# Retention and SwiGLU on one core: where stores are issued, which engine scales and copies pairs 8 to 11, and how many sums stand ahead of the first product

## The chip, the cores and the metric

The kernel runs on one NeuronCore of a Trainium2 chip, as one launch. The metric is the device time of that launch in microseconds (us). The engines are TensorE (PE; its weight loads are listed as PEld), VectorE (DVE), ScalarE (ACT), GpSimd (POOL) and SyncE (SP). SP computes nothing here, it only issues transfers; ACT issues transfers as well, between its computations. Each engine works through its own instructions in order. An instruction waits for semaphores, and whatever stands behind it on its engine waits too.

## The reference

Two blocks follow each other, all in float32.

```
B, H, S, D = 8, 8, 576, 64
scores = (q @ k.T) / sqrt(D)
ret    = scores * gamma[h] ** (i - j)  where i >= j, else 0     # gamma[h] = 1 - 2 ** (-5 - h)
x      = (ret @ v), heads side by side                          # 4608 tokens x 512
g, val = x @ w_gate, x @ w_val                                  # 512 x 1536 each
out    = (g * sigmoid(g) * val) @ w_out                         # 1536 x 512
```

## The kernel before

**Retention.** The 8 batches times 4 pairs of heads are 32 pairs, pair i = 4b + p. A sequence is cut into nine chunks of 64; within a chunk the masked scores are used, and between chunks a 64x64 state per head is carried. `tick(t)` is one beat of a pipeline over the pairs. On PE it issues, in this order, `own_values(t-2)` (masked scores times v), `new_states(t-1)` (keys times v), `earlier_values(t-2)` (state times q) and `scores(t-1)`. The work of the other engines is put into the list `pieces` and taken from it one by one by `go_on`: `masked(t-1)` gives `copies` (one copy of half the new states out of PSUM, tile `even`), `own` (mask times scores, tile `ret`) and `states` (`ret_last`, then the running sum over the chunks, tile `state`); `transposes(t)` gives `keys` (keys times their decay) and two DVE transposes of q and k; `to_x(t-2)` gives `outputs`, which move the result out of PSUM into x. Three predicates choose engines. `whole(i)` chooses a layout. `vector(i)` puts the `keys` of pair i and the `copies` one pair earlier on DVE instead of ACT, and moves `keys` behind the transposes. `light(i)` lets ACT multiply q by its decay before the transpose (`scale_q`, line 480), so that `outputs` are plain copies on ACT; for other pairs the decay is multiplied in by DVE when x is written (lines 597 and 611). `needed(1)` is 14, `needed(2)` is 22 and `FIRST` is 12.

**The feed-forward part** works on tiles of tokens. Tile 0 has 512 tokens and plain matmuls: `up0(f)` for the 12 column blocks f of w_gate and w_val (line 695), then `down0(f)` (line 707), which adds into four PSUM banks A, B, C, E, and `out0`, which copies the banks out and stores the first 512 rows. Tiles 1 to 4 have 1024 tokens each. For them a block product of 32 smaller products is done with 26, at the price of sums before and after. The tables `UP` and `DOWN` hold one line per product: the bank, the operand slots, and the sums. There are three quarters qd of 26 steps for the up side (`up_step`, four matmuls a step, line 924) and 26 steps for the down side (`down_step`, line 963). In tile 1 the sums of the weights are made on the way: `first_sums` and `w_sums` (POOL, with sign changes on ACT, lines 892, 893 and 902) before a step, after which ACT stores the summed weight block to DRAM (line 927) for tiles 2 to 4. `x_sums` makes the sums of x (DVE in tile 1, line 731 through `add`). Fourteen of tile 1's 22 sums of x stand ahead of step 0 (`X_FIRST_OF_ALL`), and one more ahead of each step. `reads` takes the result out of the bank: an ACT copy (line 861) or a DVE sum with the bank (line 864). ACT's Silu (line 939) and a product by DVE (lines 942 and 945) or POOL follow. Steps 0 to 3 and 10 and 11 are read by ACT copies, steps 4 to 9 by DVE. A line marked "+" adds onto what its bank holds: step 7 adds onto step 4's bank, step 8 onto step 5's, step 9 onto step 6's, and so on, and may begin when that bank has been read.

**The sums of w_out** (`out_sums`, table `OUT_SUMS`) are 26 operands of 128x256 for each of three quarters. Each is summed if need be (24 sums a quarter) and stored to DRAM (line 782), and is read back from there by the down steps of all later tiles. Quarters 0 and 1 are POOL's, its sums go to `pool_places` and SP stores them. The third quarter is DVE's, its sums go to `vector_places`, and ACT stores them. The 22 vector places are eight in the old x (`x0_places`, used once), six in the raw weight buffer and eight in `part`. A place whose value is no longer needed goes to the end of the list (`release`, `free`), so the 23rd and 24th sums get places that an earlier sum has used, and wait until that sum has been stored.

**Order.** Instructions of every engine stand in the order in which the Python code runs (`manual_schedule`). The loop over `down_order` calls `down0`, then `go_on(6)`; at m = 1, 3, 6 and 8 ticks 10 to 13; at m = 8 the `first_sums` of quarter 0; from m = 9 the first `x_sums`; then a group of three stores with their sums from POOL's list and a group of three from DVE's. Then come `out0`, six more `x_sums` and the 26 steps of quarter 0, with `load(12)` issued in program order after step 6 and `load(13)` after step 14. `load(i)` fetches q, k and v of pair i, ten transfers on SP; for pair 11 they are ACT's. The tile framework gives each transfer one of eight semaphores, and a transfer waits until the one before it on its semaphore has landed, whichever engine issued it.

Of the kernel before, what the change touches and what calls it, by code (L numbers as in the profile page):

```python
# [154 lines left out]
def kernel(  # L155
# [291 lines left out]

    def light(i):

        return needed(1) - 2 <= i < needed(2) - 2  # L450

    def vector(i):

        return i == 0 or 10 <= i <= needed(1) - 2

    def transposes(i):
        p = i % HP
        qk, kn, vt = loaded.pop(i)
        qT = early[i] if i < HP else qp.tile([P, S], F32, tag="qT", name="qT")
        st[i] = dict(qT=qT, kn=kn, v=vt)  # L460
        pieces = []

        copy = nc.scalar.copy if i else nc.vector.tensor_copy
        if i < HP:

            for n, (t, src, bank) in enumerate(((kT, kn, bankB), (qT, qk, bankA)) if i else ((qT, qk, bankA), (kT, kn, bankB))):
                for c in range(NFULL):
                    nc.tensor.transpose(bank[:, ts(c, P)], src[:, ts(c, P)], ident)
                for hl in range(2):
                    nc.tensor.matmul(bankC[half[hl], ts(n, L)], src[half[hl], CW : CW + D], ident[half[hl], half[hl]],  # L470
                                     start=True, stop=True, skip_group_check=True)
                copy(t[:, 0:CW], bank)
                copy(t[:, CW:S], bankC[:, ts(n, L)])
        else:
            if light(i):
                def scale_q():

                    src = qk[:, 0].rearrange("p (j r) d -> p r j d", r=2)
                    for r in range(2):
                        nc.scalar.activation(out=src[:, r], in_=src[:, r], func=AF.Copy, scale=piece[:, 2 * p + r : 2 * p + r + 1])  # L480
                pieces.append(scale_q)
            for n, t in enumerate((qT, kT)):
                pieces.append(lambda n=n, t=t: nc.vector.transpose(out=t, in_=qk[:, n].rearrange("p j d -> p (j d)")))

        every = slice(0, P)

        def keys():
            blocks = kn.rearrange("p (g d) -> p g d", d=D)
            if i < HP:
                parts = [(0, every, blocks[:, 0 : NC - 1 : 2]), (1, every, blocks[:, 1:NC:2]), (1, half[1], blocks[half[1], NC - 1])]  # L490
            elif whole(i):
                parts = [(0, every, blocks[:, 0:NFULL]), (1, every, blocks[:, NFULL:NC])]
            else:
                parts = [(hl, every, blocks[:, hl : 2 * NFULL : 2]) for hl in range(2)]
            for hl, rows, at in parts:
                scale = key[rows, 2 * p + hl : 2 * p + hl + 1]
                if vector(i) or 1 < i < HP:
                    (nc.vector if vector(i) else nc.gpsimd).tensor_scalar(out=at, in0=at, scalar1=scale, scalar2=None, op0=ALU.mult)
                else:
                    nc.scalar.activation(out=at, in_=at, func=AF.Copy, scale=scale)  # L500

        if light(i):
            return [lambda: (keys(), pieces[0]())] + pieces[1:]
        if vector(i) and i:
            return [lambda: None] + pieces + [keys]
        return [keys] + pieces

    straight, exchanged = [(slice(0, P), slice(0, P))], [(half[0], half[1]), (half[1], half[0])]
# [129 lines left out]
    def tick(t, lo=HP, hi=NP, spread=False, then=None):  # L638
        go_on(len(pieces))
        if hi == HP:  # L640

            if lo <= t - 1 < hi:
                scores(t - 1, True)
                new_states(t - 1)
                for f in masked(t - 1):
                    f()
            if t + 1 == HP:
                split(0)
                rounding(0)
            if lo <= t - 2 < hi:  # L650
                own_values(t - 2)
            for f in transposes(t) if lo <= t < hi else ():
                f()
            if t + 1 == HP:
                rounding(1)
            if lo <= t - 2 < hi:
                earlier_values(t - 2)
                to_x(t - 2)[0]()
            return
        if lo <= t - 2 < hi:  # L660
            own_values(t - 2)
        if lo <= t - 1 < hi:
            new_states(t - 1)
        if lo <= t - 2 < hi:
            earlier_values(t - 2)
        if lo <= t - 1 < hi:
            scores(t - 1, t - 2 < lo)
        if lo <= t - 1 < hi and whole(t - 2) and not whole(t - 1):
            decay(slice(0, H), slice(0, H), half[1])
        copies, *masks = masked(t - 1) if lo <= t - 1 < hi else (lambda: None,)  # L670
        keys, *new = transposes(t) if lo <= t < hi else (lambda: None,)
        outputs = to_x(t - 2)[0] if lo <= t - 2 < hi else lambda: None
        if t - 2 >= 0 and light(t - 2):
            pieces.append(lambda: (copies(), keys(), outputs()))
        else:
            pieces.extend([lambda: (copies(), keys()), outputs])
        pieces.extend(masks)
        pieces.extend(new)
        if then:
            pieces.append(then)  # L680
        if not spread:
            go_on(len(pieces))
# [25 lines left out]
                             start=(f == down_order[0]), stop=(f == down_order[-1]))  # L708

    def out0():  # L710
        for i, bank in enumerate(banks):
            o = rest[:, part_at + 512 * i : part_at + 512 * (i + 1)]
            (nc.vector.tensor_copy if i > 1 else nc.scalar.copy)(out=o, in_=bank)
        for i in range(4):
            nc.scalar.dma_start(out=out[i * P : (i + 1) * P, :], in_=rest[:, part_at + 512 * i : part_at + 512 * (i + 1)])


    up, down = lines(UP), lines(DOWN)
# [25 lines left out]
    for line in OUT_SUMS:  # L744
        i, s = line.split("|")
        slot, ops = s.split(":")
        events += [(int(op[1]), op) for op in terms(ops)] + [(None, int(slot), int(i))]

    def out_sums(qd):


        place = {}

        def free(p):
            if not any(p is q for q in x0_places):
                sum_places.append(p)

        eng, queue, sum_places = ((nc.vector, nc.scalar, vector_places) if qd + 1 == NQ else (nc.gpsimd, nc.sync, pool_places))

        def view(s):  # L760
            return w_dn[:, qd, s // 2, s % 2] if s < 8 else place[s]

        def used(e):
            return [e[1]] if e[0] is None else [int(a) for a in e[1][2:]]

        def release(k):

            for s in list(place):
                for e in events[k + 1 :]:
                    if s in used(e):  # L770
                        break
                    if s == e[0]:
                        free(place.pop(s))
                        break
                else:
                    free(place.pop(s))

        def do(k):
            e = events[k]
            if e[0] is None:  # L780
                _, slot, i = e
                queue.dma_start(out=dn_ops[i][:, qd * TB : (qd + 1) * TB], in_=view(slot))
            else:
                new = sum_places.pop(0)
                add(eng, e[1], view, new)
                if e[0] in place:
                    free(place[e[0]])
                place[e[0]] = new
            release(k)

        r, ends = [], [k for k, e in enumerate(events) if e[0] is None]
        for g in range(0, N, 3):
            lo, hi = ends[g - 1] + 1 if g else 0, ends[min(g + 2, N - 1)] + 1

            def group(lo=lo, hi=hi):
                for k in range(lo, hi):
                    do(k)

            r.append(group)
        return r  # L800
# [43 lines left out]
        rested.append(b)  # L844
        return banks[b]

    silus = [0]

    products = []

# [24 lines left out]

    x_ops = [op for line in up for op in line[3]]
    X_FIRST = 8
    X_FIRST_OF_ALL = 14

    def x_sums(n, lo, hi, vector):  # L880
        for op in x_ops[lo:hi]:
# [26 lines left out]
    def up_step(n, qd, i):  # L908
        label, opens, xslot, _, wslot, _, ops = up[i]
        busy = n == 1  # L910
        if qd == 0:
            first = X_FIRST_OF_ALL if busy else X_FIRST
            x_sums(n, first + i, first + i + 1, busy)
        if busy:
            if i > 1:
                w_sums(qd, i)
# [4 lines left out]
        b = bank(label, i == 0)  # L921
        for gv in range(2):
            for c in range(2):
                nc.tensor.matmul(b[:, gv * TB : (gv + 1) * TB], w[:, gv, ts(c, P)], rhs[:, c, :],  # L924
                                 start=(opens and gv == 0 and c == 0), stop=(c == 1), skip_group_check=True)
        if busy:
            nc.scalar.dma_start(out=up_ops[qd][i].rearrange("p (g x) -> p g x", g=2), in_=w)
            if i in (22, 25) and qd + 1 < NQ:
# [112 lines left out]
    for m, f in enumerate(down_order):  # L1041
        down0(f)
        go_on(6)
        if m in tick_at:
            tick(tick_at[m], HP, FIRST, tick_at[m] + 1 < needed(1))
            go_on(1)
        if m == 8:
            first_sums(0, 0, 4)
        if m > 8:
            x_sums(1, 3 * (m - 9), min(3 * (m - 8), X_FIRST), True)  # L1050
        if groups:
            groups.pop(0)[1]()
        if last_groups:
            last_groups.pop(0)()
    out0()
    x_sums(1, X_FIRST, X_FIRST_OF_ALL, True)
    done = FIRST

    def spread_tick(t):
# [3 lines left out]
    for n in range(1, NTILE):  # L1063
# [3 lines left out]
        if n == 1:  # L1067

            for i in range(N):
                ups.pop(0)()  # L1070
                if i in (6, 14):
                    load(FIRST + i // 14)
        downs = [lambda i=i: down_step(n, i) for i in range(N)]
        merge((0.0, ticks(done, cut)), (0.5, ups))
# [38 lines left out]
```

## Time and profile before

| what | us |
|---|---|
| median of 11 runs (lowest to highest) | 1061.25 (1059.79 to 1063.21) |
| the profiled execution's own time | 1060.36 |
| its span in the trace | 1058.6 |
| busy in the span: PE, DVE, POOL, ACT | 1038.2, 656.8, 391.3, 273.1 |
| PE from 40 to 160 us | busy throughout |
| tile 0's `up0`, then `down0` | to 124.7, then 127.3 to 179.7 |
| tile 1's first step | 180.14 |

The granted TensorE clock is 1.0 throughout. The 1.76 us between span and own time lie outside the traced instructions, and the own time is 0.89 us under the median. Times are counted from the start of the span. A line of the timeline reads: start, duration, engine (with a q: the engine's issue of transfers), line of the code, operation, what it writes and reads, count, and in brackets the engine's idle time before it and what ended that. Busy time of PE is modelled from pipelined matmuls, so that only the bracketed gaps tell where PE stood still.

### The profile page before, as it was taken

The numbers are of one execution on the slowest core, as the hardware profiler recorded it, in microseconds if no ns is written. First come the engines' busy times: TensorE is split into PE (matmuls) and PEld (weight loads), VectorE is DVE, ScalarE is ACT, GpSimd is POOL, SyncE is SP. The second block draws the span as 40 slices with busy tenths as digits, with TensorE's granted clock in tenths as the row PEclk, the third lists the DMA queues.
The fourth block names the chain that finished last, engine by engine and source line by source line (L and its number), as shares of the span: only waits on it lengthen the run. The fifth ranks groups of instructions, "written<-read, shape, count | busy, mean of one in ns | idle before, by whom it ended". The sixth has DMA issues, their size and how long they took to land.

```text
span 1058.6 us, 21426 instructions
## 1 busy us (share of the span) xinstructions
PE 1038.2 (98%) x8448; PEld 850.4 (80%) x8448; DVE 656.8 (62%) x1094; ACT 273.1 (26%) x579; POOL 391.3 (37%) x338
## 2 busy tenths in 40 slices
PE   7999999999999999999999999999999999999998
PEld 6454555788788888888888888888888888888887
DVE  4568778686878667454467787426375654244644
ACT  4555400332533211231312112232220022232110
POOL 2002357665455107622224038412250383122505
PEclk9999999999999999999999999999999999999999
DMA  9998787747768869755766777544554454555543
GB/s 264 253 255 250 183 252 208 226 159 187 189 177 218 265 168 245 212 147 173 192 189 169 210 197 212 154 145 141 157 175 150 154 187 151 152 155 161 181 159 99
DMA packets 305082, 199.08 MB, mean 188 GB/s; under 512 B 219992, under 2 KB 248664, under 8 KB 304984
## 3 DMA queue, kind: packets, MB, share of 16 engines
q1 hardware_dynamic: 269528, 157.19, 54.2%
q10 hardware_dynamic: 35456, 40.54, 11.4%
q8 instruction: 67, 1.10, 0.4%
q14 instruction: 31, 0.25, 0.1%
HBM read 157.56 MB, written 40.11 MB: 187 GB/s over the span
## 4 chain that ended last, share of the span: by engine, by line
PE 84%; DVE 6%; DMA 3%; POOL 3%; issue 2%; ACT 1%; SPq 1%; ACTq 0%; DVEq 0%; POOLq 0%
PE bankC L924 11%; PE bankA L924 11%; PE bankB L924 11%; PE bankE L924 11%; PE bankA L963 6%; PE bankE L963 6%; PE bankB L963 6%; PE bankC L963 6%; DVE rest L864 3%; PE bankA L695 2%; PE bankC L695 2%; PE bankB L695 2%; PE bankE L695 2%; POOL rest L731 2%; PE outer L546 2%
## 5 line engine op out<-in xcount | busy, mean ns | idle before, releaser
L864 POOL TENSOR_TENSOR rest<-rest 128x512 f32<-128x512 f32 x56 | 79.1, 1419 | 297.3 <-DVE rest L864 276.3
L939 ACT ACTIVATE io<-rest 128x256 f32<-128x256 f32 x180 | 75.0, 417 | 338.8 <-DVE rest L864 288.1
L924 PE MATMUL bankA<-rest,arena 128*128 128x256 f32 x544 | 129.1, 380 | 2.2 <-ACT rest L861 1.4
L924 PE MATMUL bankC<-rest,arena 128*128 128x256 f32 x544 | 129.2, 380 | 1.2 <-POOL arena L893 0.7
L731 POOL TENSOR_TENSOR arena<-arena 128x512 f32<-128x512 f32 (+1 forms) x72 | 114.3, 1600 | 26.7 <-DMA up<-arena 17.9
L924 PE MATMUL bankE<-rest,arena 128*128 128x256 f32 x512 | 121.5, 380 | 0.5 <-DVE rest L864 0.5
L924 PE MATMUL bankB<-rest,arena 128*128 128x256 f32 x512 | 121.4, 380 | 0.4 <-DVE rest L864 0.4
L924 PEld LDWEIGHTS bankA<-rest,arena 128*128 128x128 f32 x544 | 102.8, 190 | 18.1 <-issue 2.1
L924 PEld LDWEIGHTS bankC<-rest,arena 128*128 128x128 f32 x544 | 102.8, 190 | 16.3 <-issue 1.2
L946 POOL TENSOR_TENSOR arena<-rest,io 128x256 f32<-128x256 f32 x72 | 51.8, 726 | 167.5 <-ACT io L939 167.5
L924 PEld LDWEIGHTS bankE<-rest,arena 128*128 128x128 f32 x512 | 96.8, 190 | 14.6 <-DVE rest L864 0.9
L924 PEld LDWEIGHTS bankB<-rest,arena 128*128 128x128 f32 x512 | 96.9, 190 | 14.3 <-DVE rest L864 0.8
L731 POOL TENSOR_TENSOR rest<-rest 128x256 f32<-128x256 f32 (+1 forms) x66 | 67.1, 1036 | 101.0 <-DVE rest L417 58.7
L864 DVE TENSOR_TENSOR rest<-bankC,rest 128x512 f32<-128x512 f32 x72 | 48.8, 686 | 66.9 <-PE bankC L924 46.6
L864 DVE TENSOR_TENSOR rest<-bankB,rest 128x512 f32<-128x512 f32 x72 | 48.9, 687 | 65.3 <-PE bankB L924 47.3
L864 DVE TENSOR_TENSOR rest<-bankE,rest 128x512 f32<-128x512 f32 x72 | 48.8, 686 | 64.6 <-PE bankE L924 46.2
L864 DVE TENSOR_TENSOR rest<-bankA,rest 128x512 f32<-128x512 f32 x72 | 48.8, 685 | 64.5 <-PE bankA L924 46.2
L942 DVE SCALAR_TENSOR_TENSOR arena<-rest,io 128x256 f32<-128x256 f32 x84 | 56.0, 671 | 11.7 <-ACT io L939 11.7
L963 PE MATMUL bankA<-arena 128*128 128x256 f32 x252 | 58.0, 380 | 1.4 <-DVE arena L731 1.4
L963 PE MATMUL bankB<-arena 128*128 128x256 f32 x252 | 58.3, 381 | 0.0
L963 PE MATMUL bankC<-arena 128*128 128x256 f32 x252 | 58.1, 380 | 0.0
L963 PE MATMUL bankE<-arena 128*128 128x256 f32 x252 | 57.9, 379 | 0.0
(184 smaller groups left out, 1625.2 us busy)
## 6 DMA issues: line engine op xcount, KB each, us to landing
arena<-up SPq DMA_DIRECT2D x234, 256.0 KB
arena<-dn SPq DMA_DIRECT2D x104, 384.0 KB
up<-arena ACTq DMA_DIRECT2D x78, 256.0 KB
out_dram<-rest SPq DMA_DIRECT2D x32, 256.0 KB
qk<-in_q_dram SPq DMA_DIRECT2D x108, 72.0 KB
qk<-in_k_dram SPq DMA_DIRECT2D x108, 72.0 KB
dn<-rest SPq DMA_DIRECT2D x52, 128.0 KB
rest<-in_moe_w_out_dram ACTq DMA_DIRECT2D x6, 1024.0 KB
```

Of the source, the lines that this page charges most:

```text
L546: nc.tensor.matmul(xr[half[hl]] if c + 1 == NC else xo[half[hl ^ c % 2 * exchange(i)], c // 2, c % 2], state[half[hl], c, :], s["qT"][half ...
L695: nc.tensor.matmul(bank, w_up[:, f // 4, gv, f % 4, c // 2, (c % 2) * P : (c % 2 + 1) * P], xs[0][:, c, :], start=(c == 0), stop=(c == HP ...
L731: eng.tensor_tensor(out=dst, in0=srcs[0], in1=srcs[1], op=ALU.add if op[0] == "add" else ALU.subtract)
L864: eng.tensor_tensor(out=at(op[1]), in0=at(op[2]), in1=at(op[3]), op=ALU.add if op[0] == "add" else ALU.subtract)
L924: nc.tensor.matmul(b[:, gv * TB : (gv + 1) * TB], w[:, gv, ts(c, P)], rhs[:, c, :], start=(opens and gv == 0 and c == 0), stop=(c == 1), s ...
L939: nc.scalar.activation(out=s, in_=src[:, 0:TB], func=AF.Silu, scale=-1.0 if negative else 1.0)
L942: return lambda: nc.vector.scalar_tensor_tensor(out=dst, in0=src[:, TB : 2 * TB], scalar=-1.0, in1=s, op0=ALU.mult, op1=ALU.mult)
L946: nc.gpsimd.tensor_tensor(out=dst, in0=src[:, TB : 2 * TB], in1=s, op=ALU.mult)
L963: nc.tensor.matmul(b[:, m * TB : (m + 1) * TB], lhs[:, qd, ts(m, P)], w[:, qd], start=(opens and qd == 0 and m == 0), stop=(qd == NQ - 1), ...
```

## The change

1. `light` holds for pairs 8 to 19 instead of 12 to 19, and `vector` for pair 0 alone. Pairs 8 to 11 have q scaled by ACT ahead of the transpose and x copied by ACT; keys of pairs 10 to 12 and the state copies of pairs 9 to 11 go from DVE to ACT. In ticks 10 and 11 the `outputs` come right behind `copies`, and `keys` behind the masks.
2. DVE's quarter of w_out's sums is stored by SP. Its 19th and later stores are late: those straight from w_out are issued right behind the 18th store, the others behind the whole loop, and their places are not used again. In SP's order each group of three of DVE's stores stands behind the group of POOL's stores of the same m.
3. `out0` copies all four banks by ACT, into parts of `arena` that held the hidden values of tile 0, and SP stores them.
4. The sign change among the first sums of the weights stands at m = 5. Eight sums of x instead of 14 stand ahead of step 0; the other 14 follow one per step.
5. `load(12)` and `load(13)` wait on SP for the end of step 6 and of step 14 on PE.

The order of the instructions on PE and on POOL stays the same. DVE has 31 instructions fewer, SP issues 30 more transfers, ACT 30 fewer.

```diff
     def light(i):
-        return needed(1) - 2 <= i < needed(2) - 2
+        return needed(1) - 6 <= i < needed(2) - 2
     def vector(i):
-        return i == 0 or 10 <= i <= needed(1) - 2
+        return i == 0
...
         if light(i):
             return [lambda: (keys(), pieces[0]())] + pieces[1:]
-        if vector(i) and i:
-            return [lambda: None] + pieces + [keys]
         return [keys] + pieces
...
-        if t - 2 >= 0 and light(t - 2):
+        late = needed(1) - 4 <= t < needed(1) - 2
+        if late:
+            pieces.append(lambda: (copies(), outputs()))
+        elif light(t - 2):
             pieces.append(lambda: (copies(), keys(), outputs()))
         else:
             pieces.extend([lambda: (copies(), keys()), outputs])
         pieces.extend(masks)
+        if late:
+            pieces.append(keys)
         pieces.extend(new)
...
     def out0():
-        for i, bank in enumerate(banks):
-            o = rest[:, part_at + 512 * i : part_at + 512 * (i + 1)]
-            (nc.vector.tensor_copy if i > 1 else nc.scalar.copy)(out=o, in_=bank)
-        for i in range(4):
-            nc.scalar.dma_start(out=out[i * P : (i + 1) * P, :], in_=rest[:, part_at + 512 * i : part_at + 512 * (i + 1)])
+        for i, (bank, o) in enumerate(zip(banks, (hid0[f] for f in (0, 1, 4, 5)), strict=True)):
+            nc.scalar.copy(out=o, in_=bank)
+            nc.sync.dma_start(out=out[i * P : (i + 1) * P, :], in_=o)
...
+    late_stores = []
     def out_sums(qd):
+        on_time = N - 8 if qd + 1 == NQ else N
...
+        def let_go(k, s):
+            p = place.pop(s)
+            if events[k][0] is not None or stored[k] < on_time:
+                free(p)
...
-                queue.dma_start(out=dn_ops[i][:, qd * TB : (qd + 1) * TB], in_=view(slot))
+                to, what = dn_ops[i][:, qd * TB : (qd + 1) * TB], view(slot)
+                if stored[k] < on_time:
+                    nc.sync.dma_start(out=to, in_=what)
+                elif slot > 7:
+                    late_stores.append(lambda: nc.sync.dma_start(out=to, in_=what))
...
                     do(k)
+                    if stored[k] + 1 == on_time and events[k][0] is None:
+                        for _, slot, i in [e for e in events[k + 1 :] if e[0] is None and e[1] < 8]:
+                            nc.sync.dma_start(out=dn_ops[i][:, qd * TB : (qd + 1) * TB], in_=view(slot))
...
     X_FIRST = 8
-    X_FIRST_OF_ALL = 14
...
-            first = X_FIRST_OF_ALL if busy else X_FIRST
-            x_sums(n, first + i, first + i + 1, busy)
+            x_sums(n, X_FIRST + i, X_FIRST + i + 1, busy)
...
+        if m == 5:
+            first_sums(0, 0, 1)
         if m == 8:
-            first_sums(0, 0, 4)
+            first_sums(0, 1, 4)
...
+    for store in late_stores:
+        store()
     out0()
-    x_sums(1, X_FIRST, X_FIRST_OF_ALL, True)
...
                 if i in (6, 14):
+                    wait = nc.sync.nop()
+                    tc.add_manual_dep(wait.ins, stepped[-1].ins.name,
+                                      mybir.DependencyInfo(mybir.DependencyClass.Sync, mybir.DependencyReason.DATA), reason="loads in turn")
                     load(FIRST + i // 14)
```

More of the change, by code (lines that the diff above doesn't have):

```diff
@@ L756, in free @@
                 sum_places.append(p)
-        eng, queue, sum_places = ((nc.vector, nc.scalar, vector_places) if qd + 1 == NQ else (nc.gpsimd, nc.sync, pool_places))
+        eng, sum_places = (nc.vector, vector_places) if qd + 1 == NQ else (nc.gpsimd, pool_places)
         def view(s):
@@ L772, in release @@
                     if s == e[0]:
-                        free(place.pop(s))
+                        let_go(k, s)
                         break
                 else:
-                    free(place.pop(s))
+                    let_go(k, s)
         def do(k):
@@ L789, in do @@
             release(k)
+        stored = [sum(e[0] is None for e in events[:k]) for k in range(len(events))]
         r, ends = [], [k for k, e in enumerate(events) if e[0] is None]
@@ L845, in bank @@
         return banks[b]
-    silus = [0]
+    silus, stepped = [0], []
     products = []
@@ L923, in up_step @@
             for c in range(2):
-                nc.tensor.matmul(b[:, gv * TB : (gv + 1) * TB], w[:, gv, ts(c, P)], rhs[:, c, :],
-                                 start=(opens and gv == 0 and c == 0), stop=(c == 1), skip_group_check=True)
+                m = nc.tensor.matmul(b[:, gv * TB : (gv + 1) * TB], w[:, gv, ts(c, P)], rhs[:, c, :],
+                                     start=(opens and gv == 0 and c == 0), stop=(c == 1), skip_group_check=True)
+        stepped.append(m)
         if busy:
```

## The prediction

> **What bounds the kernel now.** The page first: its first part says who is busy.
>
> ```profile
> PE 1038.2 (98%) x8448; PEld 850.4 (80%) x8448; DVE 656.8 (62%) x1094; ACT 273.1 (26%) x579; POOL 391.3 (37%) x338
> ```
>
> PE is the bound, so the change can win only what PE stands still, and loses whatever new stop it causes. PE's timeline around the change shows both: the stops, and the two instructions of pair 11 that will matter.
>
> ```profile
> 167.13 0.69 PE L521 MATMUL outer<-ret,v 64*64 64x64 f32 x32
> 168.08 1.10 PE L546 MATMUL outer<-qT,state 64*64 64x64 f32 x32
> ...
> 180.14 1.99 PE L924 MATMUL bankA<-rest,arena 128*128 128x256 f32 x8 [0.46 <-ACT rest L713]
> 188.68 1.97 PE L924 MATMUL bankA<-rest,arena 128*128 128x256 f32 x8 [1.37 <-ACT rest L861]
> 198.09 1.99 PE L924 MATMUL bankE<-rest,arena 128*128 128x256 f32 x8 [0.47 <-DVE rest L864]
> 200.75 1.99 PE L924 MATMUL bankC<-rest,arena 128*128 128x256 f32 x8 [0.67 <-POOL arena L893]
> 222.48 1.75 PE L924 MATMUL bankC<-rest,arena 128*128 128x256 f32 x7 [0.53 <-DVE rest L864]
> ```
>
> From 40 to 167 us PE has no stop; between 179.7 and 222.5 it has five, 3.50 us. ACT's timeline tells why of the first two: its transfers hold its copies back.
>
> ```profile
> 134.54 43.22 ACTq L782 DMA_DIRECT2D dn<-rest  x24
> 177.81 0.63 ACT L902 ACTIVATE arena<-arena 128x512 f32<-128x512 f32 x1 [49.08 <-DMA qk<-in_q_dram]
> ...
> 187.03 0.33 ACTq L927 DMA_DIRECT2D up<-arena  x1
> 187.46 0.58 ACT L861 COPY rest<-bankA 128x512 f32<-128x512 f32 x1 [6.89 <-PE bankE L924]
> ```
>
> The copy at 187.46 was due at 182; it stood behind the issue of 187.03, which waited for the keys of `load(12)` to land (187.01 by the semaphores' updates). Last SP, whose pace will matter, in its timeline:
>
> ```profile
> 134.54 40.81 SPq L782 DMA_DIRECT2D dn<-rest  x43
> ```
>
> and in the waits of 134 to 176 us (us in all, times, longest):
>
> ```profile
> SPq L782 <- POOL rest L731: 11.8, 18, 1.4
> ...
> POOL rest L731 <- DMA dn<-rest: 13.8, 2, 13.5
> ```
>
> SP waits for POOL's sums, since POOL is far behind the program: its 29th of these 43 stores, program place m = 0, is issued at 163.91, when PE is at m = 6.
>
> **The stops that go.** ACT loses 26 stores, and `load(12)` starts after step 6. So 0.46 and 1.37 go, 1.83 together. Bank E's copy, last of four, ends 0.6 after PE's last `down0` (ACT copy of 128x512: 0.58); step 3 needs it 5.2 later. The other three stops (1.67) follow DVE and POOL. POOL's sum for step 6 waits for the first weight block to land, issued at 187.03 here and soon after 180 there, so POOL gains some 5 us against PE's 1.8 and the 0.67 probably goes. Ends 1.83 and 3.50; I take 2.5.
>
> **The new wait.** DVE's 23rd sum of w_out takes the place of its ninth, whose store is the eighth, dn6. On ACT that store is issued at 144.73 and is down by 148.4, long before DVE gets there (160 to 164). In the changed order it is SP's and stands behind 35 of POOL's stores and seven of DVE's. Behind the 23rd sum on DVE stand the mask and the states of pair 11 (lines 567 to 582 before), and for these wait PE's instructions of 167.13 and 168.08, with all of `down0` from m = 9 and the outputs of pair 11 behind them.
>
> When does dn6 land? POOL restarts at 141.60 and has the 35th store's sum at 168.64, 27.0 us. Of that 1.6 are gaps that end with a landing:
>
> ```profile
> 148.51 3.38 DMA dn<-rest
> ```
>
> That is the longest, in the chain of waits, while ACT's stores run beside it; from 155 on, with fewer beside, the semaphores give 1.7 to 2.1 per store. With ACT's stores away I let the gaps go. Another 1.1 comes from less overlap with DVE (an add of 128x256 takes POOL 0.72 alone and 0.90 beside DVE's adds), and 0.4 from an earlier restart. So the 35th sum is there at 165.5 and the 29th at 161.0. From there SP is bound by issuing: five ready stores stand at 173.09 to 174.91, 0.455 each. dn6 comes 14 issues after the 29th: 161.0 + 6.4 = 167.4, and landing 1.85 gives 169.3. Then DVE's sum (0.5) and mask and states:
>
> ```profile
> 160.56 3.15 DVE L731 TENSOR_TENSOR rest<-rest 128x256 f32<-128x256 f32 x4
> ...
> 164.56 0.67 DVE L567 TENSOR_TENSOR ret<-inner,near 128x512 f32<-128x512 f32 x1
> ...
> 167.24 0.47 DVE L582 SCALAR_TENSOR_TENSOR state<-state,tab,even 128x256 f32<-128x256 f32 x1
> ```
>
> These took 3.15 here and 2.54 a tick earlier (149.95 to 152.49); 2.7 taken. The states are ready at 172.5 against 168.08: PE stops 4.4. Low end: POOL at its uncontended pace. The 31 operations from its restart to the 35th sum (25 at 0.72, 6 at 0.85) take 23.1, so from 140.5 the 35th is there at 163.6 and the 29th at 159.3; dn6 is issued at 165.7 and lands at 167.5; with a sum of 0.4 and states of 2.54 the stop is 2.4. High end: POOL as before, 163.91 + 6.4 + 1.85 = 172.2; with 0.75 and 3.15 the stop is 8.0.
>
> [...]
>
> **Sums of x.** Six sums leave the stretch of 180 to 189, where POOL is idle, and two bank copies leave DVE too. DVE was waiting for PE at 190.75 (1.34), so this wins nothing. They come back one per step up to step 13, beside POOL:
>
> ```profile
> 182.24 0.69 DVE L731 TENSOR_TENSOR rest<-x_odd,rest 128x512 f32<-128x512 f32 x1
> 192.59 1.76 DVE L731 TENSOR_TENSOR x_odd<-rest,x_odd 128x512 f32<-128x512 f32 x1
> ```
>
> Counted from the end of step 4, DVE's reads, products and sums of steps 4 to 9 end after 15.0 us if each sum takes 1.75; step 13 may begin after 13.8. That is 1.2 late, and 0.7 more at step 16. With 1.25 a sum nothing is late. A later sum cannot help PE, so 0 is the low end; the high end is 2.5; I take 0.8, since POOL pauses in some of these steps.
>
> [...]
>
> **At no cost.** Pairs 8 to 11: DVE loses its keys, copies and multiplies (some 1.1 of x and 0.42 of copy a tick). ACT gains about 1.05 of scaling (0.525 an instruction, from later pairs), 1.0 of keys, 0.4 of copy and 1.0 of x copies: 3.5 us a tick, and ACT computes nothing from 134.5 to 164. The masks now wait for ACT's copies, some 1.5 us; PE needs them 7 us later. Without that cover each us would stop PE by one. `load(12)` and `load(13)`, 20 issues, move from 175.8 to 195.4 behind steps 6 and 14; pair 12's q is first scaled at 232, and by the semaphore order the last piece of `load(12)` follows the 11th weight store, at about 211. The four stores of `out0` end SP's queue and nothing but late products waits for them.
>
> **Sum.** 4.4 - 2.5 + 0.8 = +2.7 on the profiled execution's 1060.36 (span 1058.6 and 1.76 around it): 1063.1. The median stands 0.89 above that execution, so the forecast is 1061.25 + 2.7 = 1064.0.
>
> **Rivals.**
> - *The wait shrinks to its low end and the stops go entirely*: 2.4 - 3.5 + 0.5, about 1060.7. For it: DVE lies idle while it waits, which speeds POOL. 17%.
> - *POOL catches up, the wait never forms*: faster. If dn6 lands by 164, only the stops count, -3.0: 1058.2. POOL would have to gain 5 us or more; its uncontended pace gives 3.5 in all. Against it: the 23.1 us above. 10%.
> - *DVE becomes the bound of the first steps*: sums at 1.75 throughout and their delay carried on, or the wait at its high end: 4.4 to 8.0 - 2.0 + 2.5, about 1067. 16%.
> - *ACT isn't freed*: its weight stores share semaphores with SP's late stores; if these lag, 0.46 and 1.37 stay: 1066. SP's last late store should land by 182, before PE ends `down0`. 7%.
>
> **Numbers.** The forecast has 50%, with its own range 1062.0 to 1066.5. A difference under 0.2% (2.1 us) cannot be told from none here. Slower: 37 of the forecast's 50, 16 and 7, 0.60. Same: 13 and 17, 0.30. Faster: 0.10. The range reaches from the first rival to the third, 1060.0 to 1067.8, leaving out the second and a tail.
>
> **What would show it.** In the changed profile: a gap on PE near 167 before line 521's new place (519) and one before 544, ended by DVE, together near 4.4; DVE idle from about 160 until near 169, ended by a landing of dn; no gap before step 0 or step 4; SP issuing dn stores without a break from 161 to 178. The forecast is wrong if DVE doesn't wait there, or if gaps over 2 us appear after 190.

## The result and the profile after

The median is 1068.04 us of 13 runs (1065.36 to 1071.78) against 1061.52 of 48 runs of the kernel before; the ratio is 1.0065 with a 95% interval of 1.0053 to 1.0077. That is slower by 6.5 us by the medians and 6.9 by the ratio, where 2.7 were forecast. The profiled execution took 1070.61 (span 1068.9), 2.6 more than the median. First the busy times of the page:

```profile
PE 1041.5 (97%) x8448; PEld 852.5 (80%) x8448; DVE 652.4 (61%) x1063; ACT 284.4 (27%) x610; POOL 390.3 (37%) x338
```

PE is still the bound, but its own busy time has grown by 3.3 us with the same 8448 matmuls. Stops alone don't do that; the matmuls themselves ran slower somewhere. PE's timeline around the change:

```profile
173.24 1.13 PE L519 MATMUL outer<-ret,v 64*64 64x64 f32 x32 [5.24 <-DVE ret_last L573]
174.46 0.48 PE L540 MATMUL outer<-ret_last,v 64*64 64x64 f32 x4
174.99 1.98 PE L544 MATMUL outer<-qT,state 64*64 64x64 f32 x32
176.89 2.06 PE L710 MATMUL bankA<-rest,arena 128*128 128x512 f32 x2
...
179.65 1.02 PE L710 MATMUL bankC<-rest,arena 128*128 128x512 f32 x2
...
188.23 1.89 PE L939 MATMUL bankA<-rest,arena 128*128 128x256 f32 x8
...
211.49 1.96 PE L939 MATMUL bankE<-rest,arena 128*128 128x256 f32 x8 [0.56 <-DVE rest L881]
...
220.64 1.99 PE L939 MATMUL bankA<-x_odd,arena 128*128 128x256 f32 x8 [0.28 <-POOL arena L909]
...
229.31 1.96 PE L939 MATMUL bankC<-rest,arena 128*128 128x256 f32 x8 [1.27 <-DVE rest L881]
```

The gap is where the prediction put it, ahead of pair 11's own values, and no gap stands ahead of step 0 (188.23) any more. But look at the durations behind it: the 32 products of line 544 take 1.98 (1.10 before), the pair on bank A 2.06 (1.02 from 179.65 on). The windows of this stretch say why (start:end, length, busy times with counts, then the granted clock, DMA share and GB/s):

```profile
168.00:172.00 4.00, 0.00 (x0) 0.00 (x0) 0.11 (x1) 0.00 (x0) 3.86 (x5) 1.00 0.75 250
172.00:174.00 2.00, 0.76 (x28) 0.76 (x32) 1.93 (x6) 0.00 (x0) 0.17 (x1) 0.50 0.81 268
...
176.00:178.00 2.00, 2.00 (x20) 1.36 (x19) 0.37 (x1) 0.99 (x4) 1.27 (x1) 0.50 0.80 264
178.00:180.00 2.00, 2.00 (x5) 0.84 (x4) 1.93 (x3) 0.30 (x1) 1.62 (x1) 0.80 0.81 265
```

While PE stands still its granted clock falls from 1.00 to 0.50, and it stays there until 178.8, 5.6 us after PE has work again. DVE's and SP's timelines show the wait:

```profile
155.69 3.54 DVE L732 TENSOR_TENSOR rest<-rest 128x256 f32<-128x256 f32 x4
171.89 0.56 DVE L732 TENSOR_TENSOR rest<-rest 128x256 f32<-128x256 f32 x1 [12.66 <-DMA dn<-rest]
...
174.45 0.48 DVE L580 SCALAR_TENSOR_TENSOR state<-state,tab,even 128x256 f32<-128x256 f32 x1
```

```profile
135.32 44.12 SPq L793 DMA_DIRECT2D dn<-rest  x61
```

DVE is idle from 159.2 to 171.9, until dn6 has landed (171.80 by the semaphore's updates), with pair 11's masks and states queued behind its 23rd sum.

Where does the time go along the run? Both kernels issue the same matmuls in the same order, so the k-th of one is set against the k-th of the other; how much later it starts in the changed kernel is called the lag. The lag is 0.80 from 40 us to the seam (pair 11's own and earlier values), 8.72 behind it, 6.39 at step 4, 6.83 at 232 us, 6.95 at 345 and 10.08 from 360 to the end. So the seam costs 7.92, the stops that went bring back 2.33, and the early steps take 0.44. The 0.80 at the start and 3.1 at 354 come back below, with a second profile of the same kernel.

### The profile page after: what moved, and what is told of

Read it like the earlier page. It is cut to its first block, busy times and chain, and to the rows that moved or that the text cites. A ratio compares the mean times of both kernels' runs of the same rounds, so it can differ in the third digit from the quotient of the medians.

```text
span 1068.9 us, 21448 instructions
## 1 busy us (share of the span) xinstructions
PE 1041.5 (97%) x8448; PEld 852.5 (80%) x8448; DVE 652.4 (61%) x1063; ACT 284.4 (27%) x610; POOL 390.3 (37%) x338
## 4 chain that ended last, share of the span: by engine, by line
PE 84%; DVE 5%; POOL 3%; DMA 3%; issue 2%; SPq 1%; ACT 1%; DVEq 0%; ACTq 0%; POOLq 0%
PE bankC L939 11%; PE bankE L939 11%; PE bankA L939 11%; PE bankB L939 10%; PE bankA L979 6%; PE bankB L979 6%; PE bankC L979 6%; PE bankE L979 6%; PE bankA L698 2%; PE outer L544 2%; PE bankC L698 2%; PE bankB L698 2%; PE bankE L698 2%; DVE rest L881 2%; PE outer L519 2%
```

## The experiments

The theory: PE's stop comes from SP's order alone, and the halved clock from the stop. The rivals: DVE's sums of x, the loads held back, the work moved from DVE to ACT, or a clock that falls for another reason. Each run was timed in five rounds beside the kernel before, whose median was 1061.18 for the first four, 1061.30 for the next four and 1063.26 for the last three.

**The wait taken away: places.** Two more places for DVE's sums.

```diff
+    vector_places += [arena[:, TB * i : TB * (i + 1)] for i in range(2)]
```

> The changed kernel with two more places for DVE's sums (256 columns each, in the half of arena that held tile 0's hidden block 0), so that the 23rd and 24th sums wait for no store. Main theory (the wait for dn6 behind POOL's stores on SP, and the halved TensorE clock that follows the stop): the gap of 5.24 us ahead of line 519 goes and with it the 2.68 us that the halved clock cost, so 1068.0 - 7.9 = about 1060.1. Rival (the clock has another cause and stays low in this stretch): only 5.2 go, 1062.8. Rival (DVE's sums of x after step 0, or the loads held back behind steps 6 and 14, are what costs): 1065 or more.

Measured: 1066.30, ratio 1.0050 (1.0028 to 1.0072). By the time alone the rival that costs lie elsewhere would have won. The timeline says otherwise: no gap ahead of line 519, but a new one ahead of step 0.

```profile
168.18 0.69 PE L519 MATMUL outer<-ret,v 64*64 64x64 f32 x32
...
184.57 1.72 PE L940 MATMUL bankA<-rest,arena 128*128 128x256 f32 x6 [3.85 <-ACT arena L715]
```

```profile
183.94 0.59 ACT L715 COPY arena<-bankA 128x512 f32<-128x512 f32 x1 [12.37 <-DMA dn<-arena]
```

The place chosen was the one into which `out0` copies bank A; that copy now waited for the late store of the 24th sum. The experiment had made a second wait of the same kind, and the granted clock was 0.50 behind it too (186 to 188 us). It is mended below in places2.

**The stores back on ACT: act_stores.**

```diff
-                    nc.sync.dma_start(out=to, in_=what)
+                    (nc.scalar if qd + 1 == NQ else nc.sync).dma_start(out=to, in_=what)
```

> The changed kernel with the first 18 stores of DVE's quarter issued by ACT again; the late ones stay on SP. Main theory: dn6 lands before 150, the 23rd sum doesn't wait, no gap over 1 us ahead of line 519; ACT's copies and scalings for pairs 8 to 11 now stand between store issues, so some of the gain may be lost: 1060 to 1062. Rival (the DVE work that moved to ACT is what makes the masks of pair 11 late): the gap stays, 1066 or more.

Measured: 1061.91, ratio 1.0005 (0.9991 to 1.0019); a gap of 0.89 ahead of line 544, none ahead of line 519. The 6 us are gone, and with them part of what the change might have brought: ACT's copy of pair 11's `even` comes late between the store issues (DVE's mask waits 2.92 for it). The seam costs 1.10 of lag here.

**A stop of chosen length: stop2 and stop8.** The kernel before, with the mask of pair 11 written again (`{2, 8}` times).

```diff
         def own():
+            for _ in range({2, 8} if i == 11 else 0):
+                nc.vector.tensor_tensor(out=ret, in0=sc, in1=near[...], op=ALU.mult)
             nc.vector.tensor_tensor(out=ret, in0=sc, in1=near[...], op=ALU.mult)
```

> The kernel before, with the mask of pair 11 multiplied three times on DVE instead of once, so that its states come 1.2 us later and PE stands still by about as much once. A stop of this size (two of 1.37 and 1.38 stand in the profile before, at full clock) should cost its own length: the time before plus 1.2, about 1062.6. If any stop halves the clock: plus 3 or more.

> The kernel before, with the mask of pair 11 multiplied nine times, so that PE stands still by about 4.9 us once, at the place where the changed kernel stands still by 5.24. If the halved clock follows from the stop: a window at 0.5 of the clock after it, and plus 4.9 + 2.7 = 7.6, about 1069. If the clock of the changed kernel has another cause: plus 4.9, about 1066.3.

Measured: stop2 1063.29, ratio 1.0016 (1.0003 to 1.0029); its profile shows only 0.29 of gap there and 0.5 of lag; DVE had more slack than assumed, the rest of its time stands elsewhere (a lag of 1.07 from the start). The stop of 1.2 that was wanted did not come about, and the run tells little. stop8 1068.11, ratio 1.0063 (1.0041 to 1.0084), the changed kernel's time without any of its edits:

```profile
171.78 0.97 PE L521 MATMUL outer<-ret,v 64*64 64x64 f32 x32 [3.49 <-DVE ret_last L578]
...
174.41 1.97 PE L546 MATMUL outer<-qT,state 64*64 64x64 f32 x32 [1.11 <-DVE state L585]
176.31 2.07 PE L710 MATMUL bankA<-rest,arena 128*128 128x512 f32 x2
```

```profile
172.00:174.00 2.00, 1.23 (x36) 0.85 (x28) 1.89 (x5) 0.00 (x0) 1.56 (x2) 0.51 0.75 249
...
176.00:178.00 2.00, 2.00 (x10) 1.03 (x7) 1.57 (x7) 0.00 (x0) 0.00 (x0) 0.50 0.93 208
```

The gaps are 4.60 and the lag grows by 7.37, 2.77 more, at half clock (2.12 of it behind the start of 174.41). In this run ACT issues the stores of DVE's quarter and DVE's masks wait for no store, so the clock follows from the stop. The two stops ahead of steps 0 and 4 are gone here as well (lag 8.45 to 6.12): a late PE makes them vanish, whoever delays it.

**SP's order alone: before_sp.** One word of the kernel before.

```diff
-        eng, queue, sum_places = ((nc.vector, nc.scalar, vector_places) if qd + 1 == NQ else (nc.gpsimd, nc.sync, pool_places))
+        eng, queue, sum_places = ((nc.vector, nc.sync, vector_places) if qd + 1 == NQ else (nc.gpsimd, nc.sync, pool_places))
```

> The kernel before with one edit: the stores of DVE's quarter are issued by SP, behind POOL's of the same m, as in the changed kernel. Main theory (the wait comes from SP's order alone): a gap of 5 to 7 us ahead of the own values of pair 11 (DVE still has x of pair 10 to write behind the 23rd sum), a halved clock behind it, the stops of 0.46 and 1.37 gone: plus 6 to 8, 1067 to 1069. Rival (it takes the lighter DVE of pairs 8 to 11 to run into the wait): plus 2 or less.

Measured: 1069.21, ratio 1.0079 (1.0055 to 1.0102).

```profile
173.69 1.13 PE L521 MATMUL outer<-ret,v 64*64 64x64 f32 x32 [5.58 <-DVE ret_last L575]
```

dn6 is issued at 169.57 and lands at 171.41, within 0.4 of the changed kernel. The lag grows by 7.34 at the seam. The store's place on SP is enough to cause the wait; the lighter DVE of pairs 8 to 11 is not needed for it.

**The wait mended: places2, and its parts.** places2 is places with `out0` writing blocks 1, 4, 5 and 7. places2_x14 has 14 sums of x ahead again, places2_noturn has no waits ahead of `load(12)` and `load(13)`.

```diff
-        for i, (bank, o) in enumerate(zip(banks, (hid0[f] for f in (0, 1, 4, 5)), strict=True)):
+        for i, (bank, o) in enumerate(zip(banks, (hid0[f] for f in (1, 4, 5, 7)), strict=True)):
...
+    X_FIRST_OF_ALL = 14                                # places2_x14 only
...
-            x_sums(n, X_FIRST + i, X_FIRST + i + 1, busy)
+            first = X_FIRST_OF_ALL if busy else X_FIRST
+            x_sums(n, first + i, first + i + 1, busy)
...
     out0()
+    x_sums(1, X_FIRST, X_FIRST_OF_ALL, True)
...
-                    wait = nc.sync.nop()               # places2_noturn only
-                    tc.add_manual_dep(wait.ins, stepped[-1].ins.name, ...)
```

> As the run places, but out0 now copies into hidden blocks 1, 4, 5 and 7, so that it no longer waits for the late store of the 24th sum out of block 0 (in that run the gap of 5.24 us was gone, and one of 3.85 stood ahead of step 0 instead, ended by ACT line 715, with the halved clock behind it). Main theory: neither gap, no halved clock after 160 us: 1060 to 1061. Rival (the first steps have costs of their own, by sums of x or by late stores that hold ACT's queue): gaps of 2 us or more between 180 and 230 beyond the 1.7 of the kernel before, 1062 or more.

> As places2, with 14 sums of x ahead of step 0 again instead of 8. If the sums of x beside POOL cost 0.8 in the first steps, this is 0.8 faster than places2; if they cost nothing, no difference; if the six sums delay DVE ahead of step 0, slower.

> As places2, without the waits ahead of load(12) and load(13). Main theory: ACT's weight stores wait again on semaphores for pieces of load(12), so the stop of 1.37 ahead of step 4 comes back, plus 1.0 to 1.4 against places2. Rival (holding the loads back pays nothing, or costs at the later loads): no difference, or faster.

Measured: places2 1060.53, ratio 0.9988 (0.9973 to 1.0003). With the wait gone the changed kernel's 6.5 are gone, all of them:

```profile
166.94 0.69 PE L519 MATMUL outer<-ret,v 64*64 64x64 f32 x32
...
167.89 1.10 PE L544 MATMUL outer<-qT,state 64*64 64x64 f32 x32
```

Its lag is -0.20 ahead of the seam and -0.19 behind it, then -2.53 at step 4 and -2.12 at 232 us. places2_x14: 1059.52, ratio 0.9988 (0.9973 to 1.0002); from step 4 to 232 us its lag falls by 0.48 where that of places2 grows by 0.41, so six sums of x beside POOL cost 0.9 by the profiles. The medians differ by 1.0 and the intervals don't tell them apart. The same kernel profiled once more (best, below) falls by 0.26 there, so this price is of one profile each and no surer than some tenths. places2_noturn: 1061.25, ratio 1.0002 (0.9988 to 1.0017). The stop of 1.37 ahead of step 4 did not come back: the lag falls by 2.33 up to step 4 as in places2. Instead two stops behind POOL stand at 199.82 (1.05) and 214.95 (0.76), and from step 4 to 215 us the lag grows by 1.57 against 0.20. So holding the loads back seems to pay about 1.4, by POOL and not by ACT; one profile of each, and intervals that overlap, do not make it sure.

**The better version, its part 1, and the change once more: best, best_heavy, after_again.** best is places2_x14 again. best_heavy has `light`, `vector` and the order of `pieces` of the kernel before.

> The kernel of places2_x14 timed a second time (it was 1059.52 beside 1061.3). If its lead of about 1.7 is real, the two sets of runs together leave no difference outside; expected 1059.5 to 1060.

> As best, with part 1 of the change undone: pairs 8 to 11 have their keys, x and state copies on DVE as in the kernel before. If part 1 costs nothing and pays nothing (the prediction), no difference beyond 0.5; if DVE's lighter load is what keeps it ahead of PE from 160 to 190, a gap appears ahead of pair 11 or of step 0, plus 1 or more.

> The changed kernel itself once more, for its profile: the gap of about 5.2 ahead of line 519 and the halved clock behind it must be there again. The stops near 24 us (2.09) and 354 us (2.72), each with a halved clock, should differ from the first profile if they belong to the execution and not to the change: every kernel so far had one near 24 us, between 1.24 and 2.75.

Measured: best 1061.23, ratio 0.9983 (0.9969 to 0.9997): faster than the kernel before, by 2.0 of the medians here and 1.8 in the first set. This interval just leaves out no difference, that of the first set did not. best_heavy 1062.48, ratio 0.9994 (0.9977 to 1.0012); in its profile POOL stops PE by 0.47 and 0.87 in the first steps, and its lag at 215 us is 3.0 above best's, but the intervals overlap. after_again 1069.87, ratio 1.0063 (1.0039 to 1.0086):

```profile
174.99 1.13 PE L519 MATMUL outer<-ret,v 64*64 64x64 f32 x32 [7.25 <-DVE ret_last L573]
...
224.64 3.05 PE L939 MATMUL bankA<-x_odd,arena 128*128 128x256 f32 x8 [2.28 <-POOL arena L909]
```

The gap is there again, 2 us longer, and costs 10.18 of lag. The early steps cost 2.41 here, not 0.44 (lag 8.38 at step 4, 10.79 at 232 us): POOL's sum for the step at 224.64 is late, PE stops for 2.28, and the clock is halved behind that too (0.50 from 226 to 228 us). At the start the lag is 0.53, and the stop near 354 us is 1.77 at full clock (lag plus 0.6 instead of 3.1). So the 0.80 and most of the 3.1 of the first profile belong to that execution, not to the change.

## Why the prediction was wrong, and where it was right

**The wait: right in place, order and release.** The chain dn6, 23rd sum, mask and states, own and earlier values is in the trace as written, before_sp makes it from SP's order alone, and places2 takes it away with SP's order left as it is. The failed step is the first term of the sum, 4.4: the seam cost 7.92 in one profile and 10.18 in the other. The wait was longer than priced (earlier values 6.1 and 8.1 later), and a halved clock stood behind it (1.8 and 2.1) that had no term.

- *When dn6 lands: 169.3 forecast, 171.80 and 173.68 measured.* The 29th store was to be issued at 161.0; it was at 162.84 and 164.60 (163.91 before). Three gains were granted to POOL. The gaps that end with a landing did shrink in the first profile (0.21 left of 1.6), but in the second POOL waited 0.98 and 1.49 for landings. The earlier restart was nothing (141.71 against 141.60). The smaller overlap with DVE was nothing as well: DVE had reached its 23rd sum earlier, and its adds still fell beside POOL's up to 159 us. POOL's timeline before shows the gaps and its eight adds, 0.80 each:

```profile
148.80 2.44 POOL L731 TENSOR_TENSOR rest<-rest 128x256 f32<-128x256 f32 x3 [0.32 <-DMA dn<-rest]
152.37 0.73 POOL L728 TENSOR_TENSOR rest<-rest 128x256 f32<-128x256 f32 x1 [1.14 <-DMA dn<-rest]
...
155.62 6.41 POOL L731 TENSOR_TENSOR rest<-rest 128x256 f32<-128x256 f32 x8
```

  In the first profile after they take 0.83 each:

```profile
148.84 2.11 POOL L732 TENSOR_TENSOR rest<-rest 128x256 f32<-128x256 f32 x3 [0.21 <-DMA dn<-rest]
...
154.59 6.60 POOL L732 TENSOR_TENSOR rest<-rest 128x256 f32<-128x256 f32 x8
```

  In that profile the 35th store's sum ended at 167.31, not 165.5. From there SP was bound by issuing, as said, but 14 issues took 7.12, not 6.4 (0.51 each). Landing (1.84) and the 3.2 from landing to states (171.80 to 174.93) were right. POOL's pace lay between the forecast and the high end (POOL as before) in the first profile, and past the high end in the second.
- *What a stop costs.* Earlier values began 6.1 later, where 4.4 were forecast (174.99 against 168.08, less the 0.80 from the start). Another 1.8 came after it at half clock, 7.92 in all. The prediction counted a stop at its own length. It had no term for the clock, in any case or rival, and this holds for its low end of 2.4 too: stops of 2.28 (after_again) and 2.72 us (the changed kernel near 354) were followed by a granted clock of 0.50.

**The stops that go: 2.5 forecast, 2.33 measured** up to step 4, and that they lie so close is in part luck. The 2.33 are ACT's two stops alone, which the prediction took at the 1.83 of their brackets; by the starts of the matmuls they were worth 0.73 and 1.60. The step behind it was too narrow as well: stop8 and before_sp lose the same 2.33 merely because PE is late, and places2_noturn without the loads in turn. POOL's 0.67 did go, as forecast (lag 5.58 to 4.74 at that step), and DVE's 0.47 with it, but later stops came in their place: three gaps of 2.11 stand between 195 and 232 in the changed kernel where 1.67 stood before.

**Sums of x: 0.8 forecast, 0.9 by the profiles** of places2 and places2_x14. A stop like after_again's 2.28 is larger than this term. The prediction's sign of being wrong, gaps over 2 us after 190, did appear, once in each profile of the changed kernel and at different places (2.72 near 354, 2.28 near 224).

**At no cost:** the moved work of pairs 8 to 11 cost PE nothing at the seam (places2: lag -0.20 ahead of it, -0.19 behind it); it may even pay (best against best_heavy). ACT was freed: with the stores gone its copies for step 0 wait for PE, not for transfers:

```profile
190.20 0.59 ACT L878 COPY rest<-bankA 128x512 f32<-128x512 f32 x1 [1.19 <-PE bankA L939]
```

**The rivals.** The time is nearest to the third, 1067, by its wait at the high end and not by DVE's sums. At full clock the two profiles would be about 1.8 and 2.1 shorter, not the 2.7 and 2.9 by which the lag exceeds the gaps: earlier values wait for the states in either case (states end at 174.93 and 176.68, they begin at 174.99 and 176.74). The first term would be 6.1 and 8.1, against 4.4 with a range of 2.4 to 8.0.

## What to carry to other kernels

When a store moves to another queue, ask what stands ahead of its issue there and who reuses its source; a buffer that is used a second time makes the pace of a foreign producer (here POOL's) a wait on the engine that sums. Price a new stop of TensorE like those of 2.72 to 7.25 us here with the slow stretch behind it, which cost 0.9 (before_sp, 5.58) to 2.1 us more (stop8, after_again), and so prefer several short stops to a long one (a choice that no run here tries). Two more buffers of 256 columns, with other blocks for `out0`, took the whole loss away; the first choice of them showed that a buffer is only free if whoever needs it next comes late enough.

## What was not expected of the hardware

**The halved clock.** The stops of 2.09 (ahead of 24.12), 2.72 (ahead of 356.51) and 5.24 us in the changed kernel, 2.28 and 7.25 in after_again, 3.49 in stop8, 3.85 in places and 5.58 in before_sp each brought a granted clock of 0.50, before the stop ended or within 1.3 us of its end. The clock stayed at 1.00 behind the stops of 1.36 (ahead of 22.64) and 1.37 in the kernel before, behind after_again's 1.77 (between 356 and 360 us), and behind the 1.98 us for which PE stood still in that profile between 22 and 26 us. In the changed kernel's trace the clock was 0.50 from 25.21 to 28.62, from 171.98 to 178.81 and from 356.30 to 359.72, that is for 3.41, 6.83 and 3.41 us; these six times lie whole multiples of 3.41 us apart. What makes the clock fall behind one stop and not behind another of nearly the same length is not shown. The low stretch cost 1.6 us of lag behind 2.72 (lag 3.14, less 1.56 of longer gap) and, beyond the gaps, 1.8 (before_sp, 7.34 less 5.58) to 2.9 (after_again, 10.18 less 7.25) behind the long ones.

**The spread of a kernel's times.** In every profile, whatever the kernel, PE stands still for a while between 19 and 26 us (1.36 us ahead of 22.64 in the kernel before, 2.09 ahead of 24.12 in the changed one), and the clock is halved behind it in some (1.00 in the kernel before, 0.50 from 26 to 28 us in the changed one). In the 29 runs of the kernel before that stood beside places2, the nine at a mean clock of 1.000 took 1060.0 on average, the twelve at 0.998 took 1062.2 and the four at 0.996 took 1063.3. So a good part of what looks like noise between runs of one kernel goes with halved clock; that the early stop decides it is likely from the profiles, but where the low stretch lies in the runs without a profile is not shown.
